# Loading v of unit 1 from ScalarE's queue, with a new order for all engines

## The chip, the core and the metric

The kernel runs on one core of one Trainium2 chip. The metric is the device time of one launch in microseconds (us). The core has TensorE (PE in the profile, with its weight loads as PEld), VectorE (DVE), ScalarE (ACT), GpSimd (POOL) and SyncE (SP). A DMA is issued by an instruction in the stream of SP, ACT or POOL and is carried out by 16 DMA engines that all queues share. Semaphores tie the engines together; each engine takes its own instructions in the order in which they were written.

## What is computed

```python
# attention: B=4, H=8, S=768, D=48
for t in range(S):
    cur = einsum('bhd,bhe->bhde', u * k[:, :, t], v[:, :, t])
    y[:, :, t] = einsum('bhd,bhde->bhe', r[:, :, t], state + cur)
    state = w[None, :, :, None] * state + einsum('bhd,bhe->bhde', k[:, :, t], v[:, :, t])
# then, with x = y as (B*S, H*D) = (3072, 384):
h = maximum(x @ w_in, 0)          # w_in  (384, 2048)
out = (h * h) @ w_out             # w_out (2048, 384)
```

All inputs and the output are float32 in HBM.

## The kernel before

The sequence is cut into 6 chunks of 128 positions. A chunk of one of the 4 batches is a **unit**, 24 in all; unit i is chunk i // 4 of batch i % 4. The recurrence is done chunk by chunk as matrix products: r and k are scaled by powers of w, the 128x128 products of r and k are masked and multiplied with v, and a state for each batch carries the chunks before. The feed-forward part follows unit by unit (chunks 0 and 1) or for two units at once (chunks 2 to 5).

Nothing in the program loops over units. All work is cut into named **steps**, and a long string, `SCHEDULE`, lists 980 of them in the order in which they are written out; this list sets the order of every engine's instructions. `name:i` is the step for unit i, `n*name` repeats it, and `@b` names the PSUM bank (of 8) that it takes. The list was made by a planner, so a step's place in it is also the moment at which the planner expected it to start. A step waits by semaphore for its inputs and for its buffer or bank to be free; it cannot overtake an earlier step on the same engine.

The steps that matter here, with the engine that runs them and the lines of the profile:

- `load:i:rt`, `load:i:kt`, `load:i:vt` (L278): one DMA of r, k or v of unit i, 192 KB in pieces of 192 bytes. Units 2 to 5 are issued by POOL, all others by SP. Buffers: 3 for r, 8 for k, 4 for v.
- `weights` (L288, L291): a quarter of w_in or w_out, 384 KB as bfloat16, from POOL. The first one waits (a copy at L285) until k of unit 0 has landed.
- `scale:i:x` (L300, DVE): r (x = 0) or k (x = 1) times powers of w. `turn:i:x` (L320, PE) transposes it and `evict_rk:i:x` (L324, ACT) copies it from PSUM; from unit 6 on `turn_dma` (L309, SP) does both by a DMA transpose. `rk:i` (L329, DVE) multiplies the two.
- `at:i` (L337, PE) makes the products of r and k, `mask:i:o` (L349, DVE) masks them.
- `cast_v:i` (L304, ACT) turns v into bfloat16; `sums:i` (L357, L362, PE), `diag_v:i` (L371, DVE), `y_mm:i` (L400, L406, PE) and `evict_y:i` (L415, DVE) make y of the unit. All of them need `cast_v:i`. `state_add`, `state_decay` (DVE) and `state_cast` (ACT) carry the state.
- `x_turn:i` (L431, PE) and `evict_x:i` (L435, ACT) turn y for the feed-forward part; from unit 6 on `x_dma` (L424, SP) does so.
- `mm1:i:m:s` (L447, PE) is the first product, 12 matmuls for one unit (m = 1) or 6 wider ones for two; quarter s of w_in is its weight for m = 1. `relu` (L455, ACT) and `square` (L462 on ACT or L464 on DVE) follow, then `mm2:i:q` (L471, PE), 4 matmuls with quarter q of w_out, `evict_o` (L478, ACT) and `store` (L505).
- `fill` (L245, PE): a matmul on constant data whose result nobody reads. 68 of them stand in the early part of the list, where PE would have nothing to do.

In the list before, SP issues k0, r0, r1, k1, v0, v1, k6, k9, k7, r6 and so on, and POOL issues r2, w_in 0, k2, v2, r3, k3, w_in 1, w_in 2, v3, r4, w_in 3, r5, w_out 0, k4, w_out 1, v4, v5, k5, w_out 2, w_out 3. ACT issues one small DMA at its very start (L189, w as a row).

Of the kernel before, what the change touches and what calls it, by code (L numbers as in the profile page):

```python
# [22 lines left out]
2*fill sums:0@3 load:4:rt fill diag_v:0 turn:2:0@4 end_columns rk:1 at:1@6,7 evict_rk:2:0 evict_y:0 2*fill scale:2:1
2*fill x_turn:0@5 mask:1:1 6*fill mask:1:0 3*fill turn:2:1@1 scale:3:0 fill weights:-:3:I evict_rk:2:1 3*fill
scale:3:1 2*fill evict_x:0 fill turn:3:0@4 load:5:rt rk:2 cast_v:2 fill at:2@2,7 load:6:rt fill mask:2:0 fill
weights:-:0:O fill mm1:0:1:0@6 state_add:0 load:4:kt turn:3:1@1 relu:0:1:0 3*fill mask:2:1 fill cast_v:1 mm1:0:1:1@5
weights:-:1:O evict_rk:3:0 sums:1@2 state_cast:0 fill load:4:vt diag_v:1 sums:2@3 y_mm:1@6 relu:0:1:1 y_mm:2@7
evict_y:1 fill mm1:0:1:2@4 evict_rk:3:1 load:5:vt diag_v:2 fill rk:3 x_turn:1@5 at:3@6,1 evict_x:1 evict_y:2
load:5:kt fill relu:0:1:2 fill mask:3:0 3*fill cast_v:3 mm1:1:1:1@5 square:0:1:1:0 square:0:1:0:1 load:8:kt sums:3@7
mask:3:1 x_turn:2@4 mm1:1:1:0@6 evict_x:2 diag_v:3 relu:1:1:1 y_mm:3@1 state_add:1 weights:-:2:O mm1:2:1:2@4  # L30
relu:1:1:0 square:0:1:2:1 evict_y:3 mm1:2:1:1@5 square:1:1:0:1 state_add:3 weights:-:3:O mm1:2:1:0@6 state_add:2
x_turn:3@2 fill evict_x:3 mm1:2:1:3@1 scale:4:0 relu:2:1:2 fill mm1:1:1:3@7 relu:2:1:1 square:2:1:2:1 square:2:1:1:0
mm1:0:1:3@3 relu:2:1:0 mm1:3:1:1@2 square:2:1:0:1 mm1:3:1:3@4 relu:3:1:1 scale:4:1 mm2:1:0@5 square:1:1:1:1
relu:1:1:3 turn:4:0@6 mm2:0:0@2 relu:0:1:3 load:7:rt mm1:1:1:2@7 relu:2:1:3 evict_rk:4:0 fill turn:4:1@3 fill
mm1:3:1:0@1 evict_rk:4:1 cast_v:4 rk:4 mm2:1:1 scale:5:0 relu:1:1:2 at:4@6,0 relu:3:1:0 mm2:2:0@3 mask:4:1
state_cast:2 turn:5:0@7 mask:4:0 sums:4@1 square:1:1:2:1 mm2:0:1 scale:5:1 evict_rk:5:0 diag_v:4 y_mm:4@0 mm2:2:1
evict_y:4 turn:5:1@6 scale:6:1 mm2:0:2 evict_rk:5:1 state_add:4 square:3:1:0:1 x_turn:4@7 mm2:2:2 square:0:1:3:0
evict_x:4 square:3:1:1:1 at:5@0,6 load:6:vt mm2:3:0@1 state_cast:3 mask:5:1 mm1:4:1:0@7 square:1:1:3:0 load:8:rt
state_cast:1 rk:5 mm2:3:1 cast_v:5 mask:5:0 relu:3:1:3 mm2:0:3 square:2:1:3:0 mm1:4:1:3@6 scale:6:0 mm2:2:3
relu:4:1:3 turn_dma:6 relu:4:1:0 sums:5@0 y_mm:5@4 diag_v:5 mm1:4:1:2@6 load:8:vt scale:7:1 evict_y:5 mm1:4:1:1@7  # L40
relu:4:1:2 scale:7:0 square:4:1:0:1 mm2:1:2 state_decay:4 turn_dma:7 square:4:1:3:0 x_turn:5@4 mm2:1:3 evict_x:5
square:3:1:3:0 relu:4:1:1 mm2:4:0@6 load:7:vt evict_o:0 square:4:1:1:0 mm1:5:1:3@4 store:0:POOL load:9:rt scale:8:0
mm2:4:1 relu:5:1:3 scale:8:1 load:10:rt evict_o:1 rk:6 at:6@7,2 square:4:1:2:1 mm1:5:1:1@4 mask:6:1 cast_v:6
turn_dma:8 mm1:5:1:0@5 mask:6:0 relu:5:1:1 state_add:5 mm2:4:2 relu:5:1:0 square:5:1:1:1 mm1:5:1:2@2 sums:6@4
relu:5:1:2 mm2:4:3 diag_v:6 square:5:1:0:1 state_decay:5 y_mm:6@7 cast_v:7 rk:7 at:7@5,0 evict_y:6 square:5:1:2:1
mm2:5:0@2 mask:7:1 x_dma:6 mm1:3:1:2@7 state_add:6 mm2:5:1 relu:3:1:2 load:10:kt mask:7:0 load:9:vt sums:7@0
square:3:1:2:1 scale:9:1 mm2:5:2 evict_o:4 diag_v:7 y_mm:7@4 state_cast:4 store:4:POOL scale:9:0 at:8@7,5 evict_y:7
cast_v:8 turn_dma:9 mm2:3:2 store:1:POOL rk:8 mm1:6:1:0@6 square:5:1:3:0 x_dma:7 scale:10:0 sums:8@4 relu:6:1:0
mm2:5:3 state_add:7 mm1:6:1:1@6 evict_o:5 load:11:kt state_decay:6 square:6:1:0:1 mask:8:1 load:11:rt mm1:6:1:3@0
state_cast:5 scale:10:1 mm2:6:0@2 mask:8:0 state_cast:6 mm2:3:3 diag_v:8 turn_dma:10 relu:6:1:1 y_mm:8@5 relu:6:1:3  # L50
mm1:6:1:2@7 evict_y:8 cast_v:9 square:6:1:1:0 x_dma:8 at:9@6,0 relu:6:1:2 mm1:7:1:1@5 rk:9 square:6:1:2:1
square:6:1:3:0 sums:9@7 load:12:rt evict_o:2 mm2:6:1 mask:9:1 relu:7:1:1 load:10:vt store:2:POOL mask:9:0 mm2:6:2
store:5:POOL state_add:9 mm1:7:1:0@3 y_mm:9@0 diag_v:9 relu:7:1:0 mm1:7:1:3@5 scale:11:1 square:7:1:1:1 evict_y:9
mm1:7:1:2@6 evict_o:3 scale:11:0 square:7:1:0:1 x_dma:9 store:3:POOL mm2:6:3 relu:7:1:3 mm2:7:0@7 relu:7:1:2
square:7:1:3:0 turn_dma:11 at:10@3,0 square:7:1:2:1 state_decay:7 mm2:7:1 rk:10 mask:10:1 load:11:vt mm2:7:2
mask:10:0 load:12:kt cast_v:10 mm2:7:3 state_add:8 state_cast:7 load:13:kt sums:10@1 mm1:8:2:0@5 evict_o:6
state_decay:8 load:12:vt diag_v:10 state_cast:8 y_mm:10@6 mm1:8:2:1@0 evict_y:10 relu:8:2:0 state_decay:9
mm1:8:2:6@3 x_dma:10 relu:8:2:1 rk:11 scale:12:0 state_cast:9 at:11@4,2 mm1:8:2:2@6 mask:11:0 load:13:rt cast_v:11
mm1:8:2:5@5 square:8:2:0:1 mask:11:1 relu:8:2:2 mm1:8:2:3@0 scale:12:1 relu:8:2:6 square:8:2:1:0 turn_dma:12
sums:11@4 square:8:2:2:1 mm1:8:2:4@2 diag_v:11 relu:8:2:3 scale:13:1 mm2:8:0@6 load:14:rt relu:8:2:5 square:8:2:3:0  # L60
y_mm:11@3 square:8:2:6:1 mm2:9:0@0 evict_y:11 relu:8:2:4 scale:13:0 mm2:9:1 x_dma:11 square:8:2:5:1 state_add:11
cast_v:12 mm2:8:1 square:8:2:4:1 turn_dma:13 mm1:8:2:7@5 mm2:8:2 relu:8:2:7 load:14:kt mm2:9:2 square:8:2:7:0
load:13:vt at:12@3,2 rk:12 mm2:8:3 mask:12:1 load:15:kt sums:12@4 mask:12:0 evict_o:8 mm1:10:2:0@5 store:8:POOL
load:15:rt state_decay:11 state_add:10 y_mm:12@2 relu:10:2:0 store:6:POOL mm1:10:2:1@6 square:10:2:0:1 rk:13
load:16:rt mm1:10:2:3@3 diag_v:12 relu:10:2:1 evict_y:12 mm1:10:2:2@5 scale:14:0 x_dma:12 at:13@1,6 relu:10:2:2
square:10:2:1:0 mm1:10:2:4@2 relu:10:2:3 scale:14:1 cast_v:13 mm1:10:2:6@5 square:10:2:3:0 turn_dma:14 mm2:9:3
relu:10:2:6 mask:13:1 relu:10:2:4 sums:13@3 mask:13:0 mm1:10:2:7@5 load:14:vt square:10:2:2:1 scale:15:1
mm1:10:2:5@6 square:10:2:4:1 diag_v:13 evict_o:7 y_mm:13@2 relu:10:2:7 store:7:POOL mm2:10:0@1 evict_y:13
relu:10:2:5 scale:15:0 mm2:11:0@7 square:10:2:6:1 state_add:12 mm2:11:1 square:10:2:5:1 square:10:2:7:0 x_dma:13
mm2:10:1 state_decay:12 mm2:10:2 turn_dma:15 rk:14 at:14@5,2 state_decay:10 mm2:10:3 mask:14:1 state_cast:10  # L70
load:16:kt mm2:11:2 mask:14:0 cast_v:14 load:15:vt evict_o:9 mm1:12:2:0@6 state_add:13 load:17:rt state_cast:12
store:9:POOL y_mm:14@4 load:17:kt scale:16:0 sums:14@2 relu:12:2:0 mm1:12:2:1@5 diag_v:14 state_cast:11 mm1:12:2:2@0
evict_y:14 relu:12:2:1 state_add:14 x_dma:14 at:15@3,6 square:12:2:0:1 mm1:12:2:7@4 rk:15 state_decay:13
mm1:12:2:3@5 relu:12:2:7 scale:16:1 relu:12:2:2 mask:15:0 mm1:12:2:5@2 turn_dma:16 square:12:2:2:1 mask:15:1
mm2:11:3 cast_v:15 square:12:2:1:0 load:16:vt mm1:12:2:6@4 relu:12:2:3 state_decay:14 sums:15@0 square:12:2:3:0
relu:12:2:6 y_mm:15@3 load:18:rt evict_o:10 mm2:12:0@6 diag_v:15 state_cast:14 store:10:POOL state_add:15
mm1:12:2:4@5 relu:12:2:5 evict_y:15 mm2:13:0@4 relu:12:2:4 scale:17:0 x_dma:15 mm2:13:1 square:12:2:5:1 scale:17:1
# [480 lines left out]
```

## Time and profile before

| | before |
|---|---|
| median of 3 runs | 177.1 us (176.94 to 178.08) |
| profiled execution | 176.95 us |
| its span, first to last instruction | 175.05 us |
| outside the span | 1.90 us |
| granted TensorE clock | 1.00 throughout |
| DVE / ACT / POOL busy | 74% / 73% / 19% of the span |
| bytes moved by DMA | 28.83 MB |

The span is what the profile shows in detail; the 1.90 us lie around it. Times of the profile count from the span's start. A row of the timeline gives start, duration, engine, line, operation and operands; "SPq" and "ACTq" mark instructions that the engine's sequencer carries out itself (DMA issues, semaphore instructions), not the engine's arithmetic part. A time to landing counts from the start of the issue to the moment at which the data's semaphore is complete.

### The profile page before, as it was taken

How to read it: one execution, taken by the hardware profiler on the slowest of the kernel's cores; microseconds unless marked ns; L12 is line 12 of the kernel's file. 1: busy time of each engine (PE TensorE's matmuls, PEld its weight loads, DVE VectorE, ACT ScalarE, POOL GpSimd, SP SyncE). 2: the span in 40 equal slices, each digit the busy share in tenths (PEclk: the TensorE clock that was granted, in tenths of full speed). 3: DMA queues.
4: the chain of work that ended last, by engine and by line, in shares of the span. 5: the costliest groups of instructions: out<-in, count | busy, mean ns of one | idle time of the engine just before them, and what ended most of it. 6: DMA issues, size and time to landing. Idle time of an engine off the chain costs nothing.

```text
span 175.1 us, 4846 instructions
## 1 busy us (share of the span) xinstructions
PE 167.7 (96%) x1946; PEld 132.1 (75%) x1946; DVE 128.8 (74%) x280; ACT 128.1 (73%) x266; POOL 33.2 (19%) x66
## 2 busy tenths in 40 slices
...
DMA  5999999978595999999999998998999987521013
GB/s 109 196 221 191 215 231 249 197 139 160 108 217 106 193 159 215 198 196 155 178 236 170 230 118 188 205 131 190 207 172 170 161 165 201 112 78 35 4 45 135
DMA packets 93848, 28.83 MB, mean 165 GB/s; under 512 B 89681, under 2 KB 91730, under 8 KB 93826
## 3 DMA queue, kind: packets, MB, share of 16 engines
...
q0 software_dynamic: 4352, 9.64, 22.7%
...
q10 hardware_dynamic: 2, 0.00, 0.0%
...
## 4 chain that ended last, share of the span: by engine, by line
PE 76%; DMA 9%; ACT 6%; DVE 4%; SPq 2%; issue 1%; DVEq 0%
PE bank L447 31%; PE bank L471 30%; DMA ldv<-in_v_dram 4%; PE bank L337 4%; DMA rkT<-rkw 3%; PE bank L245 2%; PE bank L400 2%; PE bank L362 2%; ACT gr L455 2%; DMA xT<-yb 2%; SPq L278 2%; PE bank L406 2%; PE bank L486 2%; ACT g L462 1%; DVE g L464 1%; ACT osb L478 1%
## 5 line engine op out<-in xcount | busy, mean ns | idle before, releaser
L447 PE MATMUL bank<-xT,w_in_q 128*128 128x128 bf16 (+1 forms) x768 | 72.4, 246 | 0.3 <-DMA xT<-yb 0.3
L455 ACT ACTIVATE gr<-bank 128x512 f32<-128x512 f32 x96 | 53.7, 603 | 20.2 <-PE bank L447 18.9
L471 PE MATMUL bank<-w_out_q,g 128*128 128x384 bf16 x368 | 68.5, 326 | 0.0
L447 PEld LDWEIGHTS <-w_in_q 128*128 128x128 bf16 x768 | 64.1, 114 | 3.6 <-issue 0.5
L471 PEld LDWEIGHTS <-g 128*128 128x128 bf16 x368 | 33.5, 98 | 18.4
L462 ACT ACTIVATE g<-gr 128x512 bf16<-128x512 f32 x60 | 37.0, 641 | 0.4
L505 POOL DMA_DIRECT2D out_dram<-osb x21 | 11.3, 542 | 131.5 <-ACT osb L478 120.3
L349 DVE TENSOR_TENSOR am<-bank,smask 128x512 bf16<-128x512 f32 x48 | 31.5, 683 | 1.9 <-PE bank L337 1.5
L464 DVE TENSOR_TENSOR g<-gr 128x512 bf16<-128x512 f32 x36 | 24.5, 685 | 9.9 <-ACT gr L455 9.7
L371 DVE TENSOR_TENSOR dv<-vb,bank 128x384 f32<-128x384 bf16 x24 | 13.2, 549 | 7.5 <-PE bank L362 4.6
L300 DVE TENSOR_TENSOR rkw<-ldr,wpos 128x384 bf16<-128x384 f32 x24 | 13.2, 551 | 5.2 <-DMA ldr<-in_r_dram 2.6
L415 DVE TENSOR_TENSOR yb<-bank,dv 128x384 bf16<-128x384 f32 x24 | 13.3, 554 | 4.8 <-PE bank L406 4.1
L391 ACT CAST stb<-st 64x192 bf16<-64x192 f32 x40 | 13.9, 349 | 2.4 <-DVE st L385 2.0
L304 ACT CAST vb<-ldv 128x384 bf16<-128x384 f32 x24 | 12.3, 513 | 3.8 <-DMA ldv<-in_v_dram 3.5
L478 ACT COPY osb<-bank 128x384 f32<-128x384 f32 x23 | 11.0, 486 | 5.5 <-PE bank L471 5.4
L245 PE MATMUL bank<-warm 128*128 128x256 bf16 x68 | 13.6, 315 | 1.2 <-DVE warm L193 1.2
L329 DVE TENSOR_TENSOR rk<-rkT 128x512 bf16<-128x512 bf16 x24 | 10.0, 419 | 5.8 <-ACT rkT L324 4.3
L300 DVE TENSOR_TENSOR rkw<-ldk,wneg 128x384 bf16<-128x384 f32 x24 | 13.2, 550 | 0.3 <-DMA ldk<-in_k_dram 0.3
L381 DVE TENSOR_TENSOR st<-bank,st 64x192 f32<-64x192 f32 x32 | 11.2, 351 | 0.2
L324 ACT COPY rkT<-bank 128x512 bf16<-128x512 bf16 x12 | 6.9, 585 | 6.0 <-PE bank L320 5.9
L400 PE MATMUL bank<-vb,am 128*128 128x48 bf16 x192 | 8.6, 183 | 1.4 <-ACT vb L304 1.4
L400 PEld LDWEIGHTS <-am 128*128 128x128 bf16 x192 | 7.8, 96 | 2.6 <-issue 1.4
...
## 6 DMA issues: line engine op xcount, KB each, us to landing
out_dram<-osb POOLq DMA_DIRECT2D x21, 192.0 KB, 3.3
ldk<-in_k_dram SPq DMA_DIRECT2D x20, 192.0 KB, 4.0
ldr<-in_r_dram SPq DMA_DIRECT2D x20, 192.0 KB, 4.1
ldv<-in_v_dram SPq DMA_DIRECT2D x20, 192.0 KB, 4.0
...
w_out_q<-in_moe_w_out_dram POOLq DMA_DIRECT2D x4, 384.0 KB, 11.4
ldr<-in_r_dram POOLq DMA_DIRECT2D x4, 192.0 KB, 8.4
ldk<-in_k_dram POOLq DMA_DIRECT2D x4, 192.0 KB, 8.7
```

Of the source, the lines that this page charges most:

```text
L245: nc.tensor.matmul(out=bank("fill")[:, :WIDE], lhsT=warm[:, :128], rhs=warm, start=True, stop=True)
L300: nc.vector.tensor_tensor(t["rkw"][:, x, :, :, :D], pair(src), pair(wx), ALU.mult)
L349: nc.vector.tensor_tensor(am, t["at"][o], smask.unsqueeze(1).to_broadcast([C, HP, C]), ALU.mult)
L371: nc.vector.tensor_tensor(t["dv"], t["vb"], t["d"].unsqueeze(2).to_broadcast([C, H, D]), ALU.mult)
L391: nc.scalar.copy(stb[b][sl, :, o * D : (o + 1) * D], st32[b][sl])
L400: nc.tensor.matmul(out=y[:, 2 * p + o, :], lhsT=t[f"am{o}"][:, p, :], rhs=t["vb"][:, 2 * p + o, :], start=(o == 0 and p == 0), stop=c == 0 ...
L415: nc.vector.tensor_tensor(t["yb"], t["y"], t["dv"].rearrange("p h d -> p (h d)"), ALU.add)
L447: nc.tensor.matmul(out=t["h", s][:, a], lhsT=turned, rhs=chunks[c]["xT"][:, n, b : b + m, :], start=(n == 0), stop=(n == NK - 1),)
L455: nc.scalar.activation(t["gr", s], t["h", s], AF.Relu)
L462: nc.scalar.activation(g, x, AF.Square)
L464: nc.vector.tensor_tensor(g, x, x, ALU.mult)
L471: nc.tensor.matmul(out=t["o"], lhsT=chunks[units[i][0]]["g"][:, f, units[i][1], :], rhs=w_out_q[f // 4][:, f % 4, :], start=(f == 0), stop ...
```

## The change

One condition in `load` puts v of unit 1 on ScalarE's queue, and `SCHEDULE` is another list of the same 980 steps, among them the same 68 fills.

```diff
@@ load @@
-        (nc.gpsimd if i in (2, 3, 4, 5) else nc.sync).dma_start(
+        (nc.gpsimd if i in (2, 3, 4, 5) else nc.scalar if name + str(i) in ('vt1',) else nc.sync).dma_start(
@@ SCHEDULE, its start @@
 load:0:kt fill load:0:rt 2*fill load:1:rt 2*fill load:1:kt fill columns 2*fill spread_log@1 load:0:vt load:2:rt
-load:1:vt weights:kt.0:0:I fill power:0 3*fill load:2:kt power:1 scale:0:0 load:6:kt fill spread_columns@2 scale:1:0
-load:2:vt fill load:9:kt scale:0:1 2*fill copy_columns turn:0:0@3 load:3:rt fill evict_rk:0:0 turn:0:1@4 u_columns
...
+load:6:kt weights:kt.0:0:I fill power:0 3*fill load:2:kt power:1 scale:0:0 load:9:kt fill spread_columns@2 scale:0:1
+load:3:rt turn:0:0@3 copy_columns scale:1:0 turn:0:1@4 evict_rk:0:0 scale:1:1 load:3:kt load:6:rt fill load:1:vt
+2*fill turn:1:0@5 evict_rk:0:1 weights:-:1:I fill rk:0 fill at:0@6,7 load:2:vt turn:1:1@1 mask:0:1 u_columns 2*fill
+scale:2:0 fill cast_v:0 fill weights:-:2:I mask:0:0 fill evict_rk:1:0 fill load:7:kt fill sums:0@2 load:3:vt evict_rk:1:1
+fill diag_v:0 y_mm:0@3 fill scale:2:1 end_columns at:1@4,7 rk:1 fill evict_y:0 2*fill scale:3:0 3*fill x_turn:0@6
+fill evict_x:0 fill scale:3:1 2*fill turn:2:0@5 fill mask:1:1 load:4:rt evict_rk:2:0 turn:3:0@1 fill turn:2:1@3
+cast_v:1 mask:1:0 mm1:0:1:0@6 weights:-:3:I evict_rk:3:0 fill evict_rk:2:1 sums:1@5 y_mm:1@7 load:8:kt load:4:kt
+diag_v:1 relu:0:1:0 turn:3:1@4 2*fill rk:2 at:2@1,3 weights:-:0:O fill mask:2:0 3*fill cast_v:2 mm1:0:1:1@6
+load:5:rt evict_y:1 evict_rk:3:1 fill mask:2:1 fill square:0:1:0:1 2*fill x_turn:1@1 load:5:kt fill rk:3 evict_x:1
+3*fill state_add:0 sums:2@7 relu:0:1:1 y_mm:2@4 load:4:vt 2*fill mm1:1:1:0@3 diag_v:2 weights:-:1:O evict_y:2
...
```

What this makes of the queues at the start:

- **ACT**: after the two `power` steps (L253) and `evict_rk:0:0` stands the DMA of v1, then `evict_rk:0:1`, `cast_v:0`, `evict_rk:1:0` and `1:1`, `evict_x:0`, `evict_rk:2:0`, `cast_v:1`, and so on. The only wait of v1's DMA is for the landing of k0, whose semaphore it shares.
- **SP**: k0, r0, r1, k1, v0 as before, then k6, k9, r6, k7, k8, r7.
- **POOL**: r2, w_in 0, k2, r3, k3, w_in 1, v2, w_in 2, v3, r4, w_in 3, k4, w_out 0, r5, k5, v4, w_out 1, v5, w_out 2, w_out 3.
- `cast_v` of the first units comes in the order 0, 1, 2, 3; before, it was 0, 2, 1, 3.
- The last of the 68 fills stands behind 11 `mm1` steps and no `mm2` step; before, it stood behind 14 `mm1` and 2 `mm2` steps.
- The rest of the list is in another order too, all the way to the last unit; it ends with the same steps.

More of the change, by code (lines that the diff above doesn't have):

```diff
@@ L23 @@
[L23 to L77, printed above, removed]
@@ new lines @@
+fill sums:3@3 scale:4:0 fill mm1:2:1:0@5 mask:3:0 mm1:0:1:2@2 state_add:3 relu:2:1:0 weights:-:2:O fill relu:0:1:2
+fill square:0:1:1:0 mm1:2:1:1@6 square:1:1:0:1 diag_v:3 fill mm1:1:1:3@1 square:0:1:2:1 weights:-:3:O fill
+relu:1:1:3 fill mm1:2:1:2@5 square:2:1:0:1 square:1:1:3:0 y_mm:3@2 mm1:0:1:3@3 relu:2:1:2 scale:4:1 relu:1:1:1
+turn:4:0@1 evict_y:3 mm1:2:1:3@5 evict_rk:4:0 x_turn:3@4 fill evict_x:3 fill turn:4:1@2 mm2:2:0@1 evict_rk:4:1
+scale:5:0 relu:2:1:1 mm1:1:1:2@0 state_add:2 square:1:1:1:1 mm1:3:1:0@4 relu:1:1:2 square:2:1:1:0 turn:5:0@2
@@ new lines @@
+relu:2:1:3 mm2:1:0@6 relu:3:1:0 at:4@7,0 square:3:1:0:1 mm1:3:1:1@5 mask:4:1 square:2:1:2:1 mm1:3:1:3@4 scale:6:0
+square:1:1:2:1 scale:5:1 load:7:rt mm2:0:0@0 relu:0:1:3 mask:4:0 cast_v:4 mm2:2:1 rk:4 evict_rk:5:0 load:8:vt
+scale:6:1 turn:5:1@3 relu:3:1:1 mm2:1:1 evict_rk:5:1 sums:4@7 mm2:0:1 cast_v:5 state_add:4 state_cast:3 y_mm:4@2
+diag_v:4 at:5@5,3 square:3:1:1:1 evict_y:4 mm2:1:2 state_cast:1 mask:5:0 mm2:0:2 mask:5:1 x_turn:4@7 mm2:2:2
+evict_x:4 turn_dma:6 square:2:1:3:0 relu:3:1:3 mm2:3:0@2 rk:5 scale:7:1 mm1:4:1:0@5 load:6:vt square:3:1:3:0
@@ new lines @@
+sums:5@3 relu:4:1:0 y_mm:5@7 diag_v:5 state_cast:2 mm2:2:3 scale:7:0 mm2:3:1 scale:8:1 load:8:rt evict_y:5
+mm1:4:1:3@4 state_decay:4 mm1:4:1:1@5 relu:4:1:3 square:4:1:0:1 mm2:1:3 turn_dma:7 square:4:1:3:0 relu:4:1:1
+square:0:1:3:0 mm1:4:1:2@7 load:7:vt square:4:1:1:0 x_turn:5@4 relu:4:1:2 mm2:4:0@5 state_add:5 evict_x:5 mm2:0:3
+load:9:rt cast_v:6 at:6@7,4 evict_o:0 mm1:5:1:2@3 mask:6:0 square:4:1:2:1 mm1:5:1:1@0 scale:8:0 evict_o:1
+state_decay:5 store:1:POOL turn_dma:8 mm1:5:1:3@7 rk:6 rk:7 store:0:POOL mm1:5:1:0@6 relu:5:1:3 mask:6:1 load:10:rt
@@ new lines @@
+relu:5:1:2 mm2:4:1 relu:5:1:1 mm2:4:2 square:5:1:2:1 sums:6@7 relu:5:1:0 y_mm:6@4 diag_v:6 mm1:3:1:2@3
+square:5:1:0:1 evict_y:6 cast_v:7 at:7@0,6 state_add:6 x_dma:6 cast_v:8 mm2:4:3 square:5:1:1:1 mask:7:0 sums:7@4
+relu:3:1:2 mm2:5:0@7 load:9:vt scale:9:1 state_cast:4 load:10:kt mask:7:1 mm2:5:1 square:3:1:2:1 scale:9:0 mm2:5:2
+evict_o:4 rk:8 turn_dma:9 y_mm:7@0 diag_v:7 store:4:POOL mm2:3:2 evict_y:7 at:8@3,6 square:5:1:3:0 x_dma:7
+mm1:6:1:0@5 mask:8:0 sums:8@0 relu:6:1:0 state_add:7 mm2:5:3 load:11:rt square:6:1:0:1 load:11:kt mm1:6:1:1@3
@@ new lines @@
+mask:8:1 evict_o:5 diag_v:8 mm1:6:1:3@5 state_cast:5 store:5:POOL scale:10:0 y_mm:8@4 cast_v:9 scale:10:1 mm2:3:3
+relu:6:1:1 evict_y:8 turn_dma:10 mm1:6:1:2@6 square:6:1:1:0 at:9@7,3 rk:9 relu:6:1:2 x_dma:8 mm1:7:1:1@4
+state_decay:6 square:6:1:2:1 mask:9:1 mm2:6:0@6 evict_o:2 mask:9:0 load:12:rt relu:6:1:3 store:2:POOL mm2:6:1
+load:10:vt relu:7:1:1 square:6:1:3:0 mm2:6:2 sums:9@3 mm1:7:1:0@1 diag_v:9 scale:11:1 y_mm:9@7 relu:7:1:0
+state_decay:7 mm1:7:1:3@5 evict_y:9 square:7:1:0:1 mm1:7:1:2@4 rk:10 evict_o:3 x_dma:9 scale:11:0 square:7:1:1:1
@@ new lines @@
+diag_v:12 relu:10:2:1 y_mm:12@6 square:10:2:1:0 mm1:10:2:3@2 rk:13 mm1:10:2:2@5 relu:10:2:3 evict_y:12 evict_o:8
+mm1:10:2:6@3 square:10:2:3:0 x_dma:12 relu:10:2:2 store:8:POOL scale:14:1 at:13@2,6 cast_v:13 mm1:10:2:4@7
+relu:10:2:6 mask:13:1 turn_dma:14 sums:13@5 mask:13:0 relu:10:2:4 mm1:10:2:7@3 evict_o:7 scale:15:1 load:14:vt
+square:10:2:2:1 y_mm:13@6 store:7:POOL state_add:10 mm1:10:2:5@7 relu:10:2:7 store:6:POOL diag_v:13 square:10:2:6:1
+mm2:10:0@2 state_decay:11 relu:10:2:5 evict_y:13 mm2:11:0@1 square:10:2:4:1 scale:15:0 x_dma:13 mm2:11:1
@@ new lines @@
+square:10:2:5:1 square:10:2:7:0 mm2:10:1 evict_o:9 turn_dma:15 rk:14 store:9:POOL mm2:11:2 state_decay:12
+state_decay:10 mm2:10:2 state_add:13 load:16:kt mm2:10:3 load:15:vt scale:16:0 cast_v:14 load:17:rt at:14@4,3
+state_cast:12 mm1:12:2:0@7 mask:14:0 state_cast:10 mm1:12:2:1@6 load:17:kt mask:14:1 sums:14@0 relu:12:2:1 y_mm:14@5
+diag_v:14 relu:12:2:0 mm1:12:2:7@4 evict_y:14 square:12:2:0:1 mm1:12:2:5@3 rk:15 x_dma:14 state_cast:11 scale:16:1
+mm1:12:2:2@6 state_add:14 relu:12:2:7 at:15@7,5 turn_dma:16 cast_v:15 mm2:11:3 mask:15:1 relu:12:2:2 mm1:12:2:3@4
```

87 lines of the change are left out of this document (50 added, 37 removed).

## The prediction

> **What bounds the kernel now.** I read the page's totals first, then busy time by stage, for all instructions and for the fills alone.
>
> ```profile
> span 175.1 us, 4846 instructions
> PE 167.7 (96%) x1946; PEld 132.1 (75%) x1946; DVE 128.8 (74%) x280; ACT 128.1 (73%) x266; POOL 33.2 (19%) x66
> DMA  5999999978595999999999998998999987521013
> ```
> ```profile
> 20.00:35.00 15.00, 15.00 (x260) 13.77 (x259) 9.61 (x21) 14.02 (x29) 3.76 (x5) 1.00 1.10 225
> 35.00:158.00 123.00, 122.95 (x1424) 96.09 (x1424) 104.06 (x216) 97.32 (x206) 10.78 (x20) 1.00 0.91 170
> ```
> ```profile
> 20.00:35.00 15.00, 2.62 (x12) 1.09 (x12) 1.00 1.10 225
> 35.00:158.00 123.00, 0.00 (x0) 0.00 (x0) 1.00 0.91 170
> ```
>
> A row of stages gives the stage, its length, the busy time and count of PE, PEld, DVE, ACT and POOL, the granted clock, the DMA share (both at times over 1.00, as transfers overlap) and GB/s. From 35 to 158 us PE is busy for 122.95 of 123 us and runs no fill (third fence, fills alone). So nothing can be won there: both lists hold the same PE work, and the time is decided by how soon PE has only useful work, plus any new gap behind that. The fills stop at:
>
> ```profile
> 33.43 0.27 PE L245 MATMUL bank<-warm 128*128 128x256 bf16 x1
> ```
>
> Next, what delays the start. The chain of waits and the timeline of SP show it:
>
> ```profile
> 4.06 7.81 DMA ldv<-in_v_dram
> ...
> 11.89 0.51 ACT vb L304
> ...
> 14.82 0.34 PE bank L431 x3
> ```
> ```profile
> 0.74 0.46 SPq L278 DMA_DIRECT2D ldk<-in_k_dram  x1
> 1.25 1.41 SPq L278 DMA_DIRECT2D ldr<-in_r_dram  x2
> 2.71 1.30 SPq L278 DMA_DIRECT2D ldk<-in_k_dram  x1
> 4.06 2.27 SPq L278 DMA_DIRECT2D ldv<-in_v_dram  x2
> ```
> ```profile
> 4.81 1.52 SPq L278 DMA_DIRECT2D ldv<-in_v_dram  x1
> ```
>
> The DMA answers for the issues at 0.74, 2.71, 4.06 and 4.81 give these times to landing:
>
> ```profile
> ldk<-in_k_dram SPq DMA_DIRECT2D x1, 192.0 KB, 3.1
> ```
> ```profile
> ldk<-in_k_dram SPq DMA_DIRECT2D x1, 192.0 KB, 4.8
> ```
> ```profile
> ldv<-in_v_dram SPq DMA_DIRECT2D x1, 192.0 KB, 7.8
> ```
> ```profile
> ldv<-in_v_dram SPq DMA_DIRECT2D x1, 192.0 KB, 13.5
> ```
>
> k0 lands at 3.84 and k1, three loads later, at 7.51: 1.22 us per load. v0, fifth in SP's queue, lands at 11.87 (the chain's 4.06 + 7.81), and v1, sixth, at 18.3: 6.4 us for one load, since POOL's transfers have joined by then. ACT casts v0 at once (11.89), and y of unit 0 is turned at 14.82. So the kernel is bound by arrivals up to about 12 us, then by the chain over ACT and DVE, then by PE.
>
> **The step that decides: when v1 is issued.** The list puts v1's DMA behind `evict_rk:0:0` on ACT. Does ACT's sequencer wait there until that copy has run? Four rows of ACT's timeline, and the semaphore instructions that it carries out itself:
>
> ```profile
> 1.26 1.28 ACT L190 ACT_TABLE_LOAD   x1 [1.26 <-PEq L542]
> 2.56 0.52 ACT L209 ACTIVATE lnw<-wrow 1x384 f32<-1x384 f32 x1
> ...
> 17.26 0.53 ACT L304 CAST vb<-ldv 128x384 bf16<-128x384 f32 x1
> 18.93 0.60 ACT L455 ACTIVATE gr<-bank 128x512 f32<-128x512 f32 x1 [1.15 <-PE bank L447]
> ```
> ```profile
> L253 ACTq EVENT_SEMAPHORE  x1: 17/17/17, 2.0 to 2.0; - x1
> ```
> ```profile
> L455 ACTq EVENT_SEMAPHORE  x1: 17/17/17, 16.5 to 16.5; - x1
> ```
>
> The semaphore instruction of a `power` step (L253) ran at 2.0, while the table was still loading and the logarithm (L209, earlier in the order) had not begun. That of the first `relu` (L455) ran at 16.5, ahead of the cast at 17.26 that precedes it. So the sequencer passes instructions that wait for data and carries out its own when it gets to them. A DMA issue is marked ACTq too. I take it that v1 is issued not near 8 us but as soon as its only wait is over, the landing of k0: about 3.9 us, ahead of v0 on SP at 4.06. No row of before shows an ACT DMA behind waiting work; that is the open point.
>
> Then v1's pieces compete with k1 and v0 in exactly the stretch where one load costs 1.22 us, and push the end of v0 into the stretch where one costs 6.4. At best v0 loses one load at the fast pace: 11.87 + 1.22 = 13.1. At worst v0 and v1 change places: 18.3. I take 16.3, nearer to the worse end, since v1 is then wholly ahead of or beside v0 as v0 was ahead of v1, with a little off because two queues claim turns against POOL instead of one.
>
> [...]
>
> **From v0 to the last fill.** From v0's landing to the turn of its y took 14.82 - 11.87 = 2.95 us; the new list has one more `scale` in that DVE chain and two ACT copies fewer, so I keep it: x_turn:0 at 19.25. It takes 0.34, then `evict_x:0` and `evict_rk:2:0` on ACT:
>
> ```profile
> 22.37 0.48 ACT L435 COPY xT<-bank 128x384 bf16<-128x384 bf16 x1 [0.24 <-PE bank L431]
> ```
> ```profile
> L324 ACT COPY rkT<-bank 128x512 bf16<-128x512 bf16 x12 | 6.9, 585 | 6.0 <-PE bank L320 5.9
> ```
>
> with 0.48 and 0.59 that gives 20.6 for `cast_v:1`. From there to `relu:1:1:1`, which frees the bank that `x_turn:3` and the last fill wait for, the new list gives ACT 22 instructions. In 20 to 35 us before, ACT did 29 in 15 us at 14.02 busy: 0.52 each, so 11.4 us; 0.3 for the transposes behind it, and 0.7 (an estimate, about half of `diag_v` + `evict_y` + turn, 0.55 + 0.55 + 0.34) because units 1, 2 and 3 now follow one another where units 1 and 2 ran together. The last fill comes at 20.6 + 11.4 + 0.3 + 0.7 = 33.0.
>
> ```profile
> L371 DVE TENSOR_TENSOR dv<-vb,bank 128x384 f32<-128x384 bf16 x24 | 13.2, 549 | 7.5 <-PE bank L362 4.6
> L415 DVE TENSOR_TENSOR yb<-bank,dv 128x384 bf16<-128x384 f32 x24 | 13.3, 554 | 4.8 <-PE bank L406 4.1
> ```
>
> Less work is done by then: 3 `mm1`, 2 `mm2` and one `turn`, at the chain's pace
>
> ```profile
> 38.28 0.22 PE bank L320 x4
> ...
> 39.32 0.65 PE bank L471 x4
> ...
> 41.05 0.67 PE bank L447 x12
> ```
>
> 3 x 0.67 + 2 x 0.65 + 0.22 = 3.5 us. For the same end the last fill would have to come at 33.43 - 3.5 = 29.9. It comes 3.1 us late.
>
> **The other edits.** k2 keeps its place on POOL; v2 goes behind r3, k3 and w_in 1, but its cast is ACT's fifth instruction from `cast_v:1` on, at 20.6 + 4 x 0.52 = 22.7; w_in 1 comes one load sooner and is not waited for. On SP, k6, k9, r6, k7, k8 move up; none is used before the fills end. r6 takes r1's buffer early, so that r5 needs that of r3, free after `scale:3:0`, which follows `evict_y:0`: POOL may wait there to about 20 us, with k5, v4 and three quarters of w_out queued behind it, whose first use (`mm2:2:1`, `scale:5:1`) also lies behind the last fill. I cost these at nothing; the cover is gone if v2 lands after 22.7 or w_out 1 after about 37. Late in the list, PE work priced as above between `turn_dma` and `at` shrinks to 3.6 us for unit 23 (4.4 before), against
>
> ```profile
> rkT<-rkw SPq DMA_TRANSPOSE x18, 4.0
> ```
>
> so 0.4 us of new gap. Sum: 3.1 + 0.4 = 3.5; span 175.05 + 3.5 = 178.55, with 1.90 around it 180.45 us. The profiled run (176.95) is 0.15 under the median, so I compare with 177.1 as it stands: 1.9% slower.
>
> **Rivals.** *In order*: ACT issues v1 only behind `evict_rk:0:0`, near 8.3 us. v0 keeps 11.87, `cast_v:1` can run from 16.2, and v1, at 6.4 us per load, lands between 14.7 and 18.3; at 17.5 the last fill is at 17.5 + 12.4 = 29.9, nothing won or lost, 176.95 + 0.4 = 177.3 us. For it: the list was drawn up so. Against: the two ACTq rows. It decides if v1's issue starts after 7.5. *v1 early at no harm to v0*: v0 lands by 12.5, `cast_v:1` never waits, runs at 16.8, and the last fill is at 29.2 or, without the 0.7 of waits, 28.5: 0.7 to 1.4 us won less 0.4, about 176.4 us, a little faster. Against: the DMA line stands at 9s from the second slice on. It decides if v0 lands below 13.1. *ACT blocked*: SP's own issues last long once its queue is full,
>
> ```profile
> L278 SPq DMA_DIRECT2D ldk<-in_k_dram x5: 457/1632/5826, 0.7 to 13.9; - x5
> ```
>
> one of them 5.83 us, ending near 13.9. If ACT comes in order and must wait out SP's issue, `evict_rk:0:1` and `cast_v:0` slip to about 15 and v1 lands at 14.4 + 6.4 = 20.8; the last fill is at 20.8 + 12.4 = 33.2, 180.65 us. [...] No row of before shows two such issues at once.
>
> **Numbers.** Forecast 0.60, in order 0.20, no harm 0.12, blocked 0.08. Within the forecast, v0 at 13.1 gives 177.3 and at 18.3 gives 182.5. The range 176.2 to 182.6 leaves out half of "no harm" and some of the worst of the forecast, under 2 in 10. A change below 1% (175.3 to 178.9 us) is about what a measurement of this kernel can tell from none. Slower: 0.85 of the forecast, all of "blocked", 0.01 of late gaps, 0.60. Faster by over 1% needs "no harm" without waits and luck behind it: 0.05. Within 1%: 0.35.
>
> **What would show it.** v1's issue on ACT near 3.9 and not 8; k1 landing after 8.5; v1 landing before v0; ACT idle before the first cast until 16; the last fill near 33; PE full from there on. If v0's cast starts before 13, the forecast's mechanism is wrong; if the fills end before 30, its sum is.

## The result, and the profile after

After took 184.75 us (median of 4 executions, 184.12 to 185.7), before 177.17 on the same chip: 1.042 times as long, with a 95% interval of 1.036 to 1.048. The forecast was 180.4 with a range to 182.6: the sign was right, though by luck (see below), and the loss of 7.6 us was more than twice the 3.3 forecast. In the studies below some executions of a kernel, of before too (up to 183.6), run longer than the rest; a ratio leaves out those over 1.5% above the kernel's fastest, and where they are many both groups are told.

The profiled execution of after took 185.7 us with a span of 183.9. First the same totals as for before, then the same stages (all instructions, then the fills alone):

```profile
span 183.9 us, 4855 instructions
...
PE 170.7 (93%) x1946; PEld 134.4 (73%) x1946; DVE 129.3 (70%) x280; ACT 128.0 (70%) x266; POOL 32.5 (18%) x66
...
PEclk9999958999999999999999999999999999999998
```
```profile
20.00:35.00 15.00, 11.45 (x155) 10.04 (x155) 8.53 (x19) 7.57 (x16) 3.44 (x5) 0.77 1.11 225
35.00:158.00 123.00, 122.55 (x1464) 96.69 (x1463) 102.60 (x213) 96.66 (x206) 7.85 (x15) 1.00 0.89 156
```
```profile
20.00:35.00 15.00, 5.25 (x24) 2.42 (x24) 0.77 1.11 225
35.00:158.00 123.00, 1.04 (x5) 0.40 (x5) 1.00 0.89 156
```

From 35 us on PE is as full as before (122.55 of 123, of which 1.04 are the last fills). The loss lies ahead of that: in 20 to 35 us PE did 155 instructions where before did 260, it stood idle for 3.55 us, and the granted clock fell to 0.77. The list of PE's waits names what it stood for (total, times, longest), and ACT's timeline shows the same place from the other side:

```profile
PE bank L362 <- ACT vb L304: 6.5, 1, 6.5
```
```profile
5.33 0.57 ACT L253 ACTIVATE wneg<-bank,down 128x384 f32<-128x384 f32 x1
8.23 0.58 ACT L324 COPY rkT<-bank 128x512 bf16<-128x512 bf16 x1 [2.33 <-PE bank L320]
8.24 0.46 ACTq L278 DMA_DIRECT2D ldv<-in_v_dram  x1
8.74 0.58 ACT L324 COPY rkT<-bank 128x512 bf16<-128x512 bf16 x1
9.22 0.52 ACT L304 CAST vb<-ldv 128x384 bf16<-128x384 f32 x1
...
22.99 0.51 ACT L304 CAST vb<-ldv 128x384 bf16<-128x384 f32 x1 [6.87 <-DMA ldv<-in_v_dram]
```

v1's DMA (the ACTq row) was issued at 8.24, 0.01 us after `evict_rk:0:0` had begun, and not at 3.9. v0 was cast at 9.22, 2.7 us sooner than before. v1 was cast at 22.99, after ACT had stood for 6.87 us; `sums:1` (L362) waited for that cast on PE, and everything behind it on PE with it. The DMA answer for that one issue gives its time to landing:

```profile
ldv<-in_v_dram ACTq DMA_DIRECT2D x1, 192.0 KB, 14.7
```

So v1 landed at 8.24 + 14.7 = 22.9, where before it landed at 18.3. PE's timeline shows the wait, and what came after it:

```profile
16.00 0.83 PE L447 MATMUL bank<-xT,w_in_q 128*128 128x128 bf16 x12
...
23.55 0.48 PE L362 MATMUL bank<-vb,rkw 128*128 128x96 bf16 x4 [6.53 <-ACT vb L304]
...
26.50 1.49 PE L447 MATMUL bank<-xT,w_in_q 128*128 128x128 bf16 x12
...
30.07 0.83 PE L447 MATMUL bank<-xT,w_in_q 128*128 128x128 bf16 x12
```
```profile
38.78 0.38 PE L245 MATMUL bank<-warm 128*128 128x256 bf16 x2
```

The same twelve matmuls of an `mm1` took 0.83 us ahead of the gap, 1.49 after it and 0.83 again at 30: the half clock of the slices "58" in PEclk. The last fills came at 38.78.

### The profile page after: what moved, and what is told of

Its sections match the earlier page's. It is cut to its first block, busy times and chain, and to the rows that moved or that the text cites. A ratio compares the mean times of both kernels' runs of the same rounds, so it can differ in the third digit from the quotient of the medians.

```text
span 183.9 us, 4855 instructions
## 1 busy us (share of the span) xinstructions
PE 170.7 (93%) x1946; PEld 134.4 (73%) x1946; DVE 129.3 (70%) x280; ACT 128.0 (70%) x266; POOL 32.5 (18%) x66
## 4 chain that ended last, share of the span: by engine, by line
PE 76%; DMA 15%; DVE 4%; issue 1%; ACT 1%; POOL 1%; POOLq 0%; DVEq 0%
PE bank L447 32%; PE bank L471 28%; DMA ldv<-in_v_dram 8%; DMA xT<-yb 5%; PE bank L337 4%; PE bank L245 2%; DMA wu<-in_u_dram 2%; PE bank L400 2%; PE bank L362 2%; PE bank L406 2%; PE bank L486 1%; PE bank L320 1%; PE bank L357 1%; DVE yb L415 1%; DVE rkw L300 1%
## 5 line engine op out<-in xcount | busy, mean ns | idle before, releaser
L455 ACT ACTIVATE gr<-bank 128x512 f32<-128x512 f32 x96 | 54.5, 600 | 21.2 <-PE bank L447 19.9
L471 PE MATMUL bank<-w_out_q,g 128*128 128x384 bf16 x368 | 67.5, 326 | 0.0
L349 DVE TENSOR_TENSOR am<-bank,smask 128x512 bf16<-128x512 f32 x48 | 32.1, 685 | 6.0 <-PE bank L337 5.7
L245 PE MATMUL bank<-warm 128*128 128x256 bf16 x68 | 14.9, 341 | 1.2 <-DVE warm L193 1.2
L362 PE MATMUL bank<-vb,rkw 128*128 128x96 bf16 x80 | 6.8, 207 | 6.5 <-ACT vb L304 6.5
L245 PEld LDWEIGHTS <-warm 128*128 128x128 bf16 x68 | 7.3, 121 | 3.9 <-issue 1.3
L337 PE MATMUL bank<-rkT 64*128 64x128 bf16 x192 | 10.0, 226 | 0.0
```

The lines of the kernel that those rows point to most:

```text
L245: nc.tensor.matmul(out=bank("fill")[:, :WIDE], lhsT=warm[:, :128], rhs=warm, start=True, stop=True)
L337: nc.tensor.matmul(out=t["at"][o][:, p, :], lhsT=t["rkT"][sl, 1, p, :], rhs=t["rkT"][sl, 0, p, :], start=True, stop=True,)
L349: nc.vector.tensor_tensor(am, t["at"][o], smask.unsqueeze(1).to_broadcast([C, HP, C]), ALU.mult)
L455: nc.scalar.activation(t["gr", s], t["h", s], AF.Relu)
L471: nc.tensor.matmul(out=t["o"], lhsT=chunks[units[i][0]]["g"][:, f, units[i][1], :], rhs=w_out_q[f // 4][:, f % 4, :], start=(f == 0), stop ...
```

## The experiments

All are the new list (or, where said, that of before) with one or two edits. Line numbers shift by 2 in some. "Move" means that a word of `SCHEDULE` changes its place.

### v1 back on SyncE

```diff
-load:0:vt load:2:rt load:6:kt weights:kt.0:0:I
+load:0:vt load:2:rt load:1:vt load:6:kt weights:kt.0:0:I
...
-load:6:rt fill load:1:vt
+load:6:rt fill
...
-nc.scalar if name + str(i) in ('vt1',) else nc.sync
+nc.sync
```

> The new list with only v of unit 1 put back on SyncE's queue, right behind v of unit 0. Theory A (v1 is late on ScalarE's queue because it is issued at 8.2 us, in the order of the list, and from then on each queue gets one packet per turn beside GpSimd's long packets): v1 lands between 14 and 19, PE is not idle for more than 3 us before sums:1, the TensorE clock stays at 1.0, time 176.5 to 179. Theory B (the rest of the new list is slow in itself): v1 lands early too, but the time stays at 182 or above.

179.28 us (178.74 to 180.81), 1.012 times before [1.007, 1.018]: 5.5 of the 7.6 us are gone, which is v1's place alone. The time is 0.3 above theory A's range; its other signs held. ACT's and PE's rows:

```profile
17.61 0.51 ACT L302 CAST vb<-ldv 128x384 bf16<-128x384 f32 x1 [1.97 <-DMA ldv<-in_v_dram]
```
```profile
PE bank L360 <- ACT vb L302: 1.6, 1, 1.6
...
PE bank L318 <- DVE rkw L298: 1.0, 1, 1.0
```

v1 is cast 5.4 us sooner than in after, though it was issued on the queue that the change took it from. A wait of 1.0 us for `scale` (L298) is left, which the chain of waits explains:

```profile
13.29 24.22 DMA ldr<-in_r_dram
37.51 0.02 issue
37.53 1.04 DVE rkw L298 x2
```

This is r of unit 6, issued on SP at 13.29 and landed 24.2 us later. k6 and k9 stand ahead of it in SP's queue. In before they did too, and k7 with them, but there DVE came to `scale:6:0` only at

```profile
43.15 0.55 DVE L300 TENSOR_TENSOR rkw<-ldr,wpos 128x384 bf16<-128x384 f32 x1
```

while the new list has it right behind `scale:5:0`: DVE was ready for it at 35.6 here, and stood until 37.53.

### v1 early on ScalarE

```diff
-weights:kt.0:0:I fill power:0
+weights:kt.0:0:I fill load:1:vt power:0
...
-load:6:rt fill load:1:vt
+load:6:rt fill
```

> The new list with the load of v1 still on ScalarE's queue, but placed ahead of the two exponentials instead of behind evict_rk:0:0. Theory A: the issue starts at about 3.9 us (when k0 has landed), v1 lands by 13, v0 is later than in the changed kernel (9.0) by 1 to 4 us; no long PE wait, time 176 to 179.5. If the prediction's price for v0 were right (v0 at 16), time 180 to 181. Rival (ScalarE's queue is slow wherever it is issued, since it is a third queue): v1 lands 14 us or more after its issue, at 18 or later, and the time stays above 181.

179.61 us (178.6 to 180.35), 1.011 times before [1.006, 1.017]. ACT's timeline, PE's wait, and the stage behind the fills:

```profile
1.29 1.28 ACT L188 ACT_TABLE_LOAD   x1 [1.29 <-PEq L540]
2.05 0.40 ACTq L276 DMA_DIRECT2D ldv<-in_v_dram  x1
2.59 0.52 ACT L207 ACTIVATE lnw<-wrow 1x384 f32<-1x384 f32 x1
...
10.05 0.51 ACT L302 CAST vb<-ldv 128x384 bf16<-128x384 f32 x1 [0.64 <-DMA ldv<-in_v_dram]
```
```profile
PE bank L318 <- DVE rkw L298: 1.9, 1, 1.9
```
```profile
35.00:60.00 25.00, 23.06 (x284) 16.79 (x282) 17.75 (x37) 16.96 (x37) 1.10 (x2) 0.93 0.67 130
```

Here the DMA did overtake an instruction that stood ahead of it: it was issued at 2.05, the logarithm began at 2.59. (So "it cannot overtake an earlier step on the same engine", said of the steps above, did not hold for this issue, 0.54 us ahead of the logarithm.) Nor was 3.9 right, which the expectation had: k0's landing did not hold the issue here. No cast of v1 waited; the last fill came at 29.99. What was left to lose was again the wait for r6 (1.9 us), and behind it a clock of 0.93 over 25 us, some 1.7 us more. The time is 0.1 above theory A's range.

### v1 one step earlier: when does ScalarE issue?

```diff
-turn:0:1@4 evict_rk:0:0 scale:1:1 load:3:kt load:6:rt fill load:1:vt
+turn:0:1@4 load:1:vt evict_rk:0:0 scale:1:1 load:3:kt load:6:rt fill
```

> As after, with v1's load one step earlier in ScalarE's order, ahead of the first copy of rkT and behind the exponentials. Theory A (the issue comes when the ScalarE instruction ahead of it has begun): issue between 4.5 and 6 us, when the last exponential begins, v1's cast between 15 and 20 us, 179 to 183 us. Theory B (ScalarE's sequencer runs ahead and only the landing of k0 holds the issue): issue near 3.9 us. Theory C (the issue waits for transposes or for SyncE's queue): still near 8.2 us.

180.74 us (one execution).

```profile
4.85 0.58 ACT L251 ACTIVATE wpos<-bank,up 128x384 f32<-128x384 f32 x1 [1.73 <-PE bank L247]
4.86 0.40 ACTq L276 DMA_DIRECT2D ldv<-in_v_dram  x1
5.33 0.57 ACT L251 ACTIVATE wneg<-bank,down 128x384 f32<-128x384 f32 x1
```

Neither 3.9 nor 8.2. The issue came 0.01 us after `wpos` had begun, which had waited 1.73 us for PE, and ahead of `wneg`, which had nothing of its own to wait for. The first theory had the right window for a wrong reason (it said "when the last exponential begins", which was 5.33). With after (8.24 behind 8.23), the run with SyncE held (6.87 behind 6.86) and the one with GpSimd held (7.92 behind 7.91), four runs agree: v1's issue came 0.01 us after ACT had begun an instruction ahead of it in the list that had waited for PE (1.73 us here, 2.33, 0.96 and 2.01 there). `wneg` was the only instruction that the issue overtook in them. In the second experiment the logarithm was overtaken when its data had come: by the trace's semaphore records its row of w had landed at 2.02, 0.03 us ahead of the issue, and the table was still loading.

### Is it SyncE's traffic that makes v1 slow?

```diff
+    def hold():
+        nc.sync.dma_start(out=scratch, in_=tiles[1]["vt"][:, 0, :1])
...
-load:3:kt load:6:rt fill load:1:vt
+load:3:kt fill load:1:vt hold load:6:kt load:9:kt load:6:rt
```

`hold` waits on SP for v1, so k6 and what follows start after it (`load:6:kt` and `load:9:kt` move from their earlier places).

> The changed kernel, with SyncE's loads behind v0 (k6, k9, r6, k7, k8) held back by a small DMA on SyncE that waits until v1 has landed. Theory A (GpSimd's long packets set the pace of a turn, SyncE's short ones cost little): v1 lands at 19 to 22, time 181.5 to 185. Rival C (SyncE's full queue holds up ScalarE's transfer): v1's first packet follows its issue by about 1 us, as k0's did, it lands by 16, and the time falls to 177 to 179.5.

181.93 us (181.32 to 181.99), 1.025 [1.022, 1.028]. Issued at 6.87; the DMA answer:

```profile
ldv<-in_v_dram ACTq DMA_DIRECT2D x1, 192.0 KB, 13.4
```

13.4 us in place of 14.7, with SyncE's queue empty from v0 on. So SyncE's traffic is at most 1.3 us of what slows v1, as theory A had it. (Against after the time fell by 2.8 us, as v1 was cast 2.7 us sooner, at 20.25: 1.4 from the earlier issue, 1.3 from the load.)

### Is it GpSimd's?

```diff
-weights:kt.0:0:I
...
-load:6:rt fill load:1:vt
+load:6:rt fill load:1:vt u_columns weights:vt.1:0:I load:2:kt load:3:rt load:3:kt
```

GpSimd's loads from w_in 0 on are held until v1 has landed (their words move here).

> As after, but GpSimd's loads from the first quarter of w_in on are held until v1 has landed, so that v1 has only SyncE's queue beside it. Theory A (GpSimd's long pieces set the pace at which the three queues take turns): v1 lands 4 to 7 us after its issue, its cast before 15.5 us. Theory B (the ScalarE queue itself, or SyncE's full queue, is slow): 11 us or more after its issue, the cast after 19 us. The time of the whole is longer, 183 to 195 us, since the weights come later, and says nothing.

184.88 us (one execution), of no meaning by itself: PE waited 7.4 us for y of unit 0, which stood on DVE behind the scaling of k2, a load that GpSimd issues behind the hold. But the DMA answer for v1, issued at 7.92:

```profile
ldv<-in_v_dram ACTq DMA_DIRECT2D x1, 192.0 KB, 4.6
```

4.6 us in place of 14.7, while SyncE's queue moved 119 and 62 pieces per engine in 8 to 10 and 10 to 12 us. (The bound on the cast couldn't be read: `evict_x:0`, ahead of it on ACT, came only at 21.76.) The packets in the traces, counted by queue, show why. A load is 64 pieces for each of the 16 DMA engines; the table has pieces per engine in each 2 us:

```
                       8-10  10-12  12-14  14-16  16-18  18-20  20-22
before       GpSimd      20     10      5     14     22     19     13
             SyncE       26     26     42     15     14     19     13
after        GpSimd      20     11     11     17     17     16     14
             SyncE       19     22     11     17     17     16     14
             ScalarE      0      1     10     17     17     16      4
GpSimd held  GpSimd       0      0      0      8     21      9     24
             SyncE      119     62    123     20      0      0      0
             ScalarE      4     61      0      0      0      0      0
```

From 12 to 20 us of after, where all three queues had work, they moved nearly the same count, 17 : 17 : 17 in 14 to 16 and in 16 to 18. The DMA answer for 12 to 20 us of after gives the pieces of all 16 engines, their MB and the time that they took, for GpSimd (q0), SyncE (q1) and ScalarE (q10):

```profile
q0 software_dynamic: 976, 1.34, 82.8%
q1 hardware_dynamic: 976, 0.18, 20.9%
q10 hardware_dynamic: 969, 0.19, 13.4%
```

So in this stretch the queues went forward piece for piece, and most of the time was that of GpSimd's pieces: one took 0.11 us (82.8% of 16 engines' 8 us, over 976 pieces), one of SyncE's 0.03 and one of ScalarE's 0.02. At 17 pieces in 2 us, which was SyncE's count too, v1's 64 take 7.5 us; with GpSimd held 61 went in 2 us. A queue of its own thus did not make v1's pieces go faster. It did give v1 a count of its own at little cost to the others: in 14 to 20 us SyncE moved 50 pieces per engine in after and 48 in before, GpSimd 50 and 54. But v1 began no sooner for it: its first piece went at 11.45 us, 3.2 us after the issue (1.9 with GpSimd held; what the time before the first piece goes to is not shown). In before SyncE's queue had moved the 320 pieces per engine up to the end of v0 by 9.6 us, in the mean of the engines, and went on to v1. There v1 also met a pause of GpSimd at 12 to 14 us (SyncE moved 42 pieces), which after did not have (11).

### The half clock

```diff
-sums:1@5
+45*fill sums:1@5
```

> The changed kernel with 45 more fills ahead of sums:1, about 5 to 6 us of PE work in the stretch in which PE waits for v1. If the halved TensorE clock after that wait costs time: the granted clock stays at 1.0 to 35 us, the time falls by 1 to 3 us, to 182 to 183.8. If ScalarE and VectorE alone set the pace behind the wait: the time stays within 0.7 us of the changed kernel's 184.75.

183.87 us (182.92 to 184.12), 1.036 [1.032, 1.040]. The time fell by 0.9 us, just short of the 1 to 3 of the first theory and more than the 0.7 of the second.

```profile
20.00:35.00 15.00, 13.73 (x228) 12.71 (x226) 10.10 (x22) 10.43 (x22) 3.45 (x5) 1.00 1.12 227
```
```profile
35.90 0.38 PE L243 MATMUL bank<-warm 128*128 128x256 bf16 x2
```

The fills keep PE busy up to 1.3 us before `sums:1`, the clock stays at 1.00, and the last fill comes 2.9 us sooner than in the profile of after, 0.5 of it because v1's cast does (22.48); by the medians 0.9 us of the loss is the half clock.

### r of unit 6 in front of k of unit 9

```diff
-scale:0:0 load:9:kt fill
+scale:0:0 fill
...
-load:3:kt load:6:rt
+load:3:kt load:6:rt load:9:kt
```

Once on the kernel with v1 early on ScalarE:

> As the run with v1's issue ahead of the power steps, with one more edit: k of unit 9 goes behind r of unit 6 in SyncE's queue. In that run PE waited 1.9 us at 36.5 for the scaling behind r of unit 6, which landed at 37.4, and its clock then ran at half pace for 3.4 us. Theory A (these two are what is left of the loss): r of unit 6 lands near 28, no such wait, no half clock; 179.6 less 1.9 less 1.7 is 176.0, range 175.5 to 177.3 us. Theory B (the rest of the new list, its later gaps, is the loss): 178.3 to 179.8 us.

and once on that with v1 on SyncE:

> As the run with v1 on SyncE right behind v0 and r2, with one more edit: k of unit 9 goes behind r of unit 6 in SyncE's queue, so that r6 comes one load of 192 KB sooner. Theory A (the wait for r6, 1.0 us in that run, is the larger part of what the new order still lost): no wait for r6, 177.3 to 178.6 us. Theory B (the later part of the new order loses the 2.1 us): 178.9 to 179.8 us as before the edit. Theory C (the run's start is set by v0 against GpSimd's pieces, with or without ScalarE's queue): executions of 180 us and more among them.

With v1 on SyncE: 177.73 us over 12 executions, ten of them 176.0 to 178.0, one 178.7 and one 183.0; 1.000 times before [0.998, 1.003]. PE's waits for ACT and DVE after the start are only

```profile
PE bank L360 <- ACT vb L302: 1.6, 1, 1.6
...
PE bank L429 <- DVE yb L413: 0.2, 1, 0.2
```

so the 1.0 for r6 is gone and with it the last of the loss. It was close: DVE still waited for r6, which landed at 36.9, only 0.6 us sooner: SyncE's queue moved few pieces while GpSimd had loads (48 beside GpSimd's 48, of all 16 engines, in 15.0 to 15.3 us here; in after 10 per engine in 2 us from 24 to 32 us, beside GpSimd's 10, and 87 from 36 to 38, beside 1). The last part of the new list loses nothing that can be measured.

With v1 on ScalarE the executions fall in two groups: eight of 14 at 176.5 to 178.1 (1.000 times before), six at 180.3 to 183.8. The profile is of one at 183.65, and shows what the forecast feared. ACT, the DMA answer for v0 (issued at 3.53), and PE:

```profile
18.22 0.51 ACT L302 CAST vb<-ldv 128x384 bf16<-128x384 f32 x1 [8.30 <-DMA ldv<-in_v_dram]
```
```profile
ldv<-in_v_dram SPq DMA_DIRECT2D x1, 192.0 KB, 14.7
```
```profile
PE bank L360 <- ACT vb L302: 5.8, 1, 5.8
```

v0 was pushed from 9 to 18.2 us, as in the forecast's worst case of 18.3; that the two agree so closely is chance. With v1 between, 60 of the 320 pieces that SyncE's queue had for each engine up to v0 were left at 8 us, when GpSimd's pieces came in number (in after 5 per engine in 6 to 8 us and 20 in 8 to 10, while SyncE's count fell from 62 to 19).

### Before's list with v1 on ScalarE

The one condition in `load`, nothing else; in this list v1 stands early, ahead of `power:0`.

> The order of before, word for word; only the queue of v1's load is ScalarE's, where it is the first thing that the order asks of ScalarE after the logarithm. Theory A (a load gets about one turn in three or two whichever queue it is in, and what counts is that it is queued early and nothing waits behind it): v1 is issued near 2 us, lands by 7, the cast of v0 stays below 12.5, cast of v1 no longer waits; PE was busy for 16.5 of the first 20 us, so little is to be won: 175.5 to 177.2 us. Theory B (the third queue itself harms the loads on SyncE: v0 is pushed to 13 or later): v0's cast after 13, last fill after 33.4, 178 to 181 us.

One execution, the profiled one, at 178.28 us with v0's cast at 12.41; five at 183.3 to 184.4. That fits neither theory: one time in the second's range but with v0 cast as in the first, five above both. So the queue alone costs about 6 us most times. That these five are v0 pushed back, as above, is likely but was not traced.

### Taking GpSimd out of the race

If v0 races GpSimd's pieces, holding w_in 0 until v0 has landed should steady the time.

```diff
-weights:kt.0:0:I
+weights:vt.0:0:I
```

On the list with v1 early and k9 behind r6, on before's list with v1 on ScalarE, on before itself, and on the new list with v1 on SyncE and k9 behind r6:

> As the run with v1 early on ScalarE and k9 behind r6, with one more edit: GpSimd's first load of w_in is held until v of unit 0 has landed (before, until k of unit 0 has). In that run v of unit 0 had 60 of its 320 pieces per DMA engine left when GpSimd's pieces began in earnest, and in the profiled execution it landed at 18.2 us, in others the time was that of a kernel with no such wait. Theory A (it is a race between the end of v0 and the begin of GpSimd's pieces): v0's cast before 10 us in every execution, no execution above 179 us, median 175.5 to 177.3 us. Theory B (the third queue itself makes it unsteady): some executions again at 180 to 184 us.

> The order of before with v1 on ScalarE's queue, early, and w_in's first load held until v of unit 0 has landed. Theory A (race of v0 with GpSimd's pieces): v0's cast before 10 us, no execution above 179 us, median 175.3 to 177.0 us. Theory B (the third queue makes it unsteady, or SyncE's queue is slowed by it): most executions again at 182 to 184 us.

> Before, with only w_in's first load held until v of unit 0 has landed; v1 stays on SyncE. Theory A: v0's cast near 9.2 in place of 11.9, v1 lands before 15 in place of 18.3 us; PE has at most 3.5 us of idle time in its first 20 us to lose, 175.0 to 177.0 us. Theory B (the fills in the order set the start whatever lands when, or w_in comes too late): 176.8 to 178.5 us.

> The new order with v1 on SyncE right behind v0 and r2, k9 behind r6, and w_in's first load held until v0 has landed: what the new order is worth without ScalarE's queue. Theory A (r6 and v1's landing were all that the new order lost): v1's cast without a wait, near 16 us, no wait for r6, 175.5 to 177.3 us. Theory B (the later part of the new order loses too): 177.8 to 179.5 us.

| | median of 6 | from, to | ratio to before |
|---|---|---|---|
| new list, v1 early on ScalarE | 182.72 | 181.05, 183.56 | 1.029 [1.024, 1.034] |
| before's list, v1 on ScalarE | 179.96 | 179.72, 180.64 | 1.016 [1.012, 1.019] |
| before | 180.39 | 179.57, 183.34 | 1.018 [1.012, 1.023] |
| new list, v1 on SyncE | 181.28 | 180.28, 182.21 | 1.023 [1.018, 1.027] |

v0's cast speaks for the race: it came at 10.65, 10.68, 9.75 and 9.41, in the order of the table, where the profiles without the hold had 18.22, 12.41, 11.89 and 9.31. (The first two are above the 10 forecast.) In before's list with v1 on ScalarE the times became steady, six executions within 0.5%, where without the hold five of six were 5 us longer than the sixth; in the other three lists they still spread by 1 to 2%, which is not explained. No time came out as expected, since the hold costs 3 to 6 us of its own. In the list with v1 early, PE's longest wait is new:

```profile
PE bank L355 <- POOL uwb L265: 3.7, 1, 3.7
```

`uwb` is computed by GpSimd itself, behind the hold in its stream. With v1 on SyncE this wait was 3.5 us; in the two lists of before it was under 1, and what the hold costs there stays open. None of these beat before, nor did any other run here.

## Why the prediction was wrong

**What bounds the kernel** stood: PE is full from 35 us on, and the start decides.

**"I take it that v1 is issued not near 8 us but as soon as its only wait is over, the landing of k0: about 3.9 us, ahead of v0 on SP at 4.06."** This step failed: the issue came at 8.24. The two rows it rested on were read as DMA-like instructions passing work that waited for data. In both, the work passed had its data and only stood in line: behind the table load at 2.0, and at 16.5 behind a copy that another row of before's timeline shows beginning at 16.41,

```profile
16.41 0.59 ACT L324 COPY rkT<-bank 128x512 bf16<-128x512 bf16 x1 [2.15 <-PE bank L320]
```

after a wait of 2.15 us: the semaphore instruction of `relu` came at 16.46, 0.05 us behind the end of that wait, as v1's DMA came 0.01 us behind one in four runs.

**v0 pushed to 16.3** hung on that step and did not happen in after (v0 cast at 9.22). What came late was v1, the load that the forecast had ahead of v0: the sign was right by luck, for the forecast's loss and the measured one belong to two different loads. Why v0 was cast 2.7 us sooner than in before is seen in part. In before the issue of k1 took 1.30 us and that of v0 began at 4.06; in after

```profile
2.77 0.71 SPq L278 DMA_DIRECT2D ldk<-in_k_dram  x1
3.52 1.18 SPq L278 DMA_DIRECT2D ldv<-in_v_dram  x1
```

In the profiles in which GpSimd was not held and no piece of v1 went on ScalarE's queue before 10 us, v0's issue at 3.51 to 3.61 went with a cast at 9.17 to 9.49 (after, 45 fills, v1 on SyncE with k9 in both places), and at 3.93 and 4.06 with 11.32 and 11.89 (SyncE held, before). Half a microsecond thus seems to decide whether v0 is through before GpSimd's pieces; why k1's issue takes longer in some is not shown. The push itself was seen: with v1's issue at 2.05 v0 was cast at 10.05, with 2.06 at 18.22. In that last profile the turn of its y began at 21.73, 3.5 us behind v0's landing, where the sum had 2.95; the clock was half there.

**From `cast_v:1` to the last fill, 12.4 us**, was 15.8 in after (22.99 to 38.78). At full clock it was 13.4 with the 45 fills (22.48 to 35.90) and 13.4 with v1 on SyncE (17.61 to 31.03): the term was 1.0 too small, and the half clock was not in the sum.

**The parity of 29.9** was right to 0.1 us in three profiles, without the 0.4 of late gaps. After: last fill 38.78, 8.9 late, span 175.05 + 8.9 = 183.95, measured 183.9. With 45 fills: 35.90, 6.0 late, 181.05, measured 181.1. With v1 on SyncE: 31.03, 1.1 late, and 1.0 for r6, 177.15, measured 177.2. Its 3.5 us of work was 3.3: behind the last fill PE was busy for 137.5 us in before and 140.8 in after.

**The other edits at nothing.** In after this held, as everything came too late for them to matter. But "none is used before the fills end" missed r6, asked for some 4 us behind them (35.6, with the last fill at 31.03): once v1 is early, r6 behind k9 is what is left of the loss, 1.6 us by the two medians with v1 on SyncE (179.28 to 177.73). The 0.4 of new gaps late in the list did not show: from the last fill to its last matmul PE stood idle for 0.45 us in after and 0.37 in before.

**The rival "in order"** had the right issue and the wrong price. It put v1's landing at 14.7 to 18.3, from "6.4 us per load"; it was 22.9. That price was of a load already at the head of SyncE's queue when GpSimd paused. Of the 14.7 us that it took here, some 3 went before the first piece and the rest at one piece in three (17 beside 17 and 17 in 2 us). "ACT blocked" did not occur. SyncE's issue of 5.83 us in before did begin with 2235 pieces of 192 bytes, over two loads, still ahead of it in its queue, and ended with 1853 left, its own among them; but v1's issue took 0.46 us while SyncE's issue of r6 ran from 8.35 to 14.39, and `evict_rk:0:1` went at 8.74. "v1 early at no harm" came about only with the issue moved ahead, in some executions, and won nothing there: 1.000 times before with k9 behind r6.

So the 7.6 us: 5.5 for v1's place, of which 0.9 half clock (by the medians), and 2.1 for the rest of the new list, of which moving one load took away 1.6 and left nothing that can be told from before.
